# Streaming the last 96 columns of w1 beside the third block of wqkv, under a written-out order, in a transformer block with local attention and an MLP gate

## The chip, the cores and the metric

The kernel runs on one core of one Trainium2 chip. The metric is the device time of one execution in microseconds, the median over several runs. A profile of one execution comes with it: its span is the time between the first and the last thing that the profiler saw, and the time of the execution lies a little above that. The engines are TensorE (PE, with its weight loads apart as PEld), VectorE (DVE), ScalarE (ACT), GpSimd (POOL) and SyncE (SP, which here issues nearly all DMAs).

## The reference

```python
x = A_x                                   # 1 x 2048 x 512, f32
xn = layernorm(x)
qkv = (xn @ wqkv)                         # wqkv 512 x 1536; 32 heads of 16
# local attention: position s looks at s, s-2, ..., s-14 (8 offsets, dilation 2)
logits[s, w] = q[s] . k[s - 2 w] / 4      # -1e9 where s - 2 w < 0
o[s] = sum_w softmax(logits)[s, w] v[s - 2 w]
s = o @ wo                                # wo 512 x 512
y = layernorm(xn)
g = silu(gelu_tanh(y @ w1 + b1) @ w2 + b2)  # w1 512 x 1376, w2 1376 x 512
return x + s * g
```

## The kernel before, in words

**Matmuls in halves.** Each f32 factor is scaled by a power of two and split into a high and a low f16 half. A product is three f16 matmuls (high x high, low x high, high x low) summed in PSUM, over KT = 4 slices of the 512 input features: 12 matmuls for a tile of 128 tokens.

**Tokens and units.** Since the dilation is 2, even and odd positions never meet in the attention. The 2048 tokens are two parities c of 1024, each 8 tiles i of 128. The heads form NHB = 4 blocks hb of 8 heads, so wqkv falls into four blocks of 3 x 128 = 384 columns. One *unit* is a pair (c, hb): `qkv(c, hb, u)` multiplies the 8 tiles of a parity by a block of wqkv, 8 x 12 matmuls of 384 columns (L746), and ACT or DVE evicts each tile into one of two buffers U (L763, L759). SP then copies shifted rows (the halo) inside U. `attention(c, hb, u)` works on DVE with some help of POOL: multiply q with shifted k (L805), reduce (L808), softmax, multiply with shifted v (L863), sum (L858, L873, L883), scale into o (L846, L848), transposed by DMA into oT. There are eight units, four of parity 0 and four of parity 1.

**The MLP** works on four chunks ch of 512 tokens. `mlp1(ch, f)` makes 128 rows of the hidden layer for 512 tokens, f = 0 to NF - 1 = 10: 12 matmuls (L1016) with w1 as the stationary side, gelu on ACT (L1033), high half on ACT (L1036), low half on DVE (L1038). w1 has 1376 = 10 x 128 + 96 columns, so f = 10 has 96 rows (FL = 96) and goes into a tile of its own, `hlast`, whose row 97 is a constant for the bias b2. `mlp2(ch, f)` multiplies the hidden rows with w2, 4 tiles x 3 matmuls of 512 columns (L1052), summed over f in four PSUM banks z. For parity 0 the gates silu(z) go to DRAM (gd) and come back; for parity 1 they stay in U.

**The end.** wo is applied to the first three head blocks as oT comes in (L929), and for parity 1 at the end (L961). The DVE then forms gate x product (L993) and adds x (L1000, or on POOL L997), and SP writes the tile (L1002). The last tile is worked in two halves of 256 columns.

**What sets the order.** Every operation is added to a `Plan` with its engine, an estimated duration, what it reads and writes and a priority. `issue()` then picks, again and again, the operation that can start earliest, by priority among those within a small window, and emits it. The instructions of an engine, SP's DMAs among them, then run in the order in which they were emitted, each behind semaphores for what it reads. The head of the program loads x, transposed x, wqkv and the MLP weights in the order of `LOADS`; tables at the top say which engine does which cast, which tiles are transposed by DMA (`BYDMA`) or on PE (L683), and in what groups the layernorm statistics are worked (`GROUPS`).

Of the kernel before, what the change touches and what calls it, by code (L numbers as in the profile page):

```python
# [18 lines left out]
P = 128  # L19
S, D, F = 2048, 512, 1376  # L20
H, DH, W, DIL = 32, 16, 8, 2
KT = D // P
# [16 lines left out]
LAG = 2  # L39

# [4 lines left out]
BYDMA = (4, 5, 6, 7)  # L45
TRZ = (3, 3, 0, 2, 0, 1, 1, 0)
PTR = (0.5487, 0.3388, 0.0342, 0.6565, 0.7826, 0.1978, 0.0549, 0.9)
GROUPS = ((0,), (1, 2), (3, 4, 5), (6, 7))
BATCHES = ((0, 1, 2, 3, 4, 5), (6, 7))
LOADS = (('t', 6), ('q', 0), ('q', 2), ('x', 2), ('x', 0), ('q', 4), ('t', 7), ('x', 5), ('x', 1), ('x', 3), ('x', 4), ('q', 6), ('w', 0), ('w', 2), ('x', 7), ('c', 2), ('s', 1), ('c', 0), ('w', 3), ('x', 6), ('w', 1), ('c', 1), ('b', 0), ('s', 0))  # L50
HI_ENG = ('act', 'act', 'act', 'dve', 'dve', 'dve', 'dve', 'act')
XT = (0, 4, 30, 34)
Y_ENG = ('pool', 'act', 'dve', 'dve', 'act', 'pool', 'dve', 'act')

W1ENG = ('act', 'dve', 'act', 'act', 'act', 'act', 'act')
# [3 lines left out]
W2LO = ('dve', 'dve', 'dve', 'dve', 'dve', 'pool', 'dve')  # L59
EV0 = ('act', 'dve', 'dve', 'act', 'act', 'act', 'dve', 'dve')  # L60
EV1 = ('dve', 'dve', 'act', 'act', 'act', 'act', 'dve', 'act')
QLO0 = ('pool', 'dve', 'dve', 'pool')
QLO1 = ('dve', 'dve')
W1LO = ('dve', 'dve', 'pool', 'dve', 'dve', 'dve', 'dve')
WOLAG = 2
MEANBY = ('dve', 'pe', 'pool', 'pool')
W2LATE = 6

BEFORE_W1 = (0, 1, 4, 5)

# [26 lines left out]
class Plan:  # L97
# [9 lines left out]
    def add(self, eng, dur, fn, reads=(), writes=(), prio=None, table=None, nbytes=0,  # L107
            after=None, holds=(), port=False, rate=350e3, issue=0.55, tail=1.4):
# [56 lines left out]
    def start(self):  # L165
        for o in self.ops:
            o.npred, o.ready, o.succs = len(o.preds), 0.0, []
        for o in self.ops:
            for p in o.preds:
                p.succs.append(o)  # L170
        self.free = {o.eng: 0.0 for o in self.ops}
        self.portfree, self.dma, self.landed, self.table = 0.0, 0.0, [], None

    def earliest(self, o):
# [3 lines left out]
        if o.eng == "sp" and o.nbytes:  # L178
            left = FLIGHT
            for end, n in reversed(self.landed):  # L180
                left -= n
                if left < 0:
                    t = max(t, end)
                    break
        return t

    def place(self, o, t):

        if o.eng == "sp":
# [3 lines left out]
            self.dma = max(self.dma, t + o.issue + 0.3)  # L193
            self.dma += o.nbytes / (o.rate if self.dma > SLOW else 265e3)
            end = self.dma + o.tail
            self.landed.append((end, o.nbytes))
            return end
        end = t + o.dur
        if o.nbytes:
            self.free[o.eng] = end  # L200
            self.dma = max(self.dma, end + 0.3) + o.nbytes / o.rate
            return self.dma + o.tail
# [19 lines left out]
    def issue(self):  # L222
# [5 lines left out]
        order = []  # L228
        while len(order) < len(self.ops):
            best = None  # L230
            for e, cand in engs.items():
# [46 lines left out]
SLOW = 5.5  # L278

FLIGHT = 0.9e6  # L280

PW2 = 1.1284
PS2 = 0.4252
PWQ1 = 0.9
PW1 = 0.423
PB1 = 0.75
PCS = 0.6
PQ0 = 0.2677
PSQ0 = 0.1788
# [12 lines left out]
PS1 = 1.1561
# [3 lines left out]
PQLO = 0.5225  # L306

PFPLN = 0.35
PSEC = (0.6153, 0.7518, 0.1)

U1MH = 4
# [5 lines left out]
IORD0 = (6, 7, 0, 4, 1, 3, 2, 5)  # L317
IORD1 = (7, 0, 6, 3, 2, 4, 5, 1)
MLPN = (7, 7, 6, 4, 7, 7, 2, 0)
# [7 lines left out]
def tile_mixer(ctx, tc, a_x, a_xt, a_wqkv, a_wo, b_w1, b_b1, b_w2, out):  # L327
# [34 lines left out]
    ident = sb.tile([P, P], F32, name="ident")  # L362
    make_identity(nc, ident)
    fours = sb.tile([P, 2 * P], BF16, name="fours")
    nc.vector.memset(fours, 4.0)
    mean1 = sb.tile([P, P], F32, name="mean1")
# [9 lines left out]
    wq = sb.tile([P, NHB, 2, KT, 384], F16, name="wq")  # L376
    w1 = sb.tile([P, 2, KT * F], F16, name="w1")
# [6 lines left out]
    b1T = sb.tile([P, NF], F32, name="b1T")  # L384
    hlast = sb.tile([P, 2, 512], F16, name="hlast")
# [81 lines left out]
    def low_pool(n, lo, get, s, hi, **k):  # L467
# [4 lines left out]
        pool(0.45 + n * 3.9e-3, fn, **k)  # L472
# [25 lines left out]
    def k0(hb):  # L498
        return dict(rate=400e3, tail=0.6, issue=0.45) if hb == 0 else dict(tail=3.5) if hb > 1 else {}
# [9 lines left out]
    def scale_q(hb):  # L509
        col = R_s.new()  # L510
        for k in range(0, KT, 2):
            def go(k=k):
                src = stq[hb]()[:, k * 384:(k + 2) * 384]
                nc.scalar.activation(wq[:, hb, 0, k:k + 2].bitcast(BF16),
# [11 lines left out]
    def prep_q(hb):  # L526
# [3 lines left out]
        for k in range(0, KT, st):  # L530
            n = st * 384
            dst = [wq[:, hb, t, k:k + st].rearrange("p k e -> p (k e)") for t in range(2)]
            src = lambda k=k, n=n: stq[hb]()[:, k * 384:k * 384 + n]
# [17 lines left out]
    def factors(n, V, vs, mk, cdst, ckeys):  # L551
# [12 lines left out]
            rb.t[:, 0:n], p0b.t[:, 0:n], halves[:, 0:n], op=ALU.pow), [p0b], [(rb, 0)], port=False)  # L564
        with pl.fuse():
# [5 lines left out]
            cdst, a1(), halves[:, 8:8 + n], op=ALU.pow), [(A, 1)], ckeys, port=False)  # L571
# [53 lines left out]
    def ln0(g):  # L625
        q, n = cpos[g[0]], len(g)
        for i in g:
# [8 lines left out]
            rb0[:, q:q + n], pb0[:, q:q + n], halves[:, 0:n], op=ALU.pow), [("pb", g)], [("rb", g)], port=False)  # L636

    def second(g):
# [4 lines left out]
        with pl.fuse():  # L643
# [5 lines left out]
            cT[:, 0, q:q + n], x1, halves[:, 8:8 + n], op=ALU.pow), [("ab", g)], [("c", 0, i) for i in g], port=False)  # L649

    def y0(i):
# [12 lines left out]
        elif Y_ENG[i] == "pool":  # L664
            pool(1.25, lambda: nc.gpsimd.tensor_scalar(x(), x(), mv0[:, q, 0:1], rb0[:, q:q + 1], op0=ALU.subtract,
# [4 lines left out]
        if i in BYDMA:  # L670
# [6 lines left out]
                [y16, (y16, 0)] + [k for n in range(4) for k in s1k[n]], [("yh", 0, i), ("y", 0, i)], rate=140e3, issue=1.6, tail=1.2)  # L677
# [14 lines left out]
    def ln1():  # L692
# [13 lines left out]
        for i in range(NI):  # L706
# [10 lines left out]
                [y16, (y16, 0)], [("y", 1, i), ("yT", 2 + i // 4)], rate=1e6, issue=1.3)  # L717

# [646 lines left out]
```

## Time and profile before

| | before |
|---|---|
| median of 3 runs | 415.14 us (414.89 to 415.17) |
| the profiled execution | 415.18 us, span 413.4 us, mean granted clock 0.999 |
| busy: PE, DVE | 405.9 us, 379.5 us |
| busy: ACT, POOL | 222.1 us, 120.3 us |
| DMA traffic | 46.41 MB, 112 GB/s on average |
| first qkv matmul, last matmul | 15.96 us, to 409.78 us |

Busy time is the time in which an engine has an instruction under way. The chain of waits follows back from the last instruction what released it, or else the instruction ahead of it on its engine; the pieces of that chain add up to the span. In the groups, a row gives line, engine, operation, tiles and shapes, the count, then total busy time in us and mean ns, then the idle time ahead and who ended it. The table of stages gives start:end and length, the busy time of PE, PEld, DVE, ACT and POOL, the granted clock, the busy share of the DMA engines and GB/s.

### The profile page before, as it was taken

The numbers are of one execution on the slowest core, as the hardware profiler recorded it, in microseconds if no ns is written. First come the engines' busy times: TensorE is split into PE (matmuls) and PEld (weight loads), VectorE is DVE, ScalarE is ACT, GpSimd is POOL, SyncE is SP. The second block draws the span as 40 slices with busy tenths as digits, with TensorE's granted clock in tenths as the row PEclk, the third lists the DMA queues.
The fourth block names the chain that finished last, engine by engine and source line by source line (L and its number), as shares of the span: only waits on it lengthen the run. The fifth ranks groups of instructions, "written<-read, shape, count | busy, mean of one in ns | idle before, by whom it ended". The sixth has DMA issues, their size and how long they took to land.

```text
span 413.4 us, 5554 instructions
## 1 busy us (share of the span) xinstructions
PE 405.9 (98%) x2083; PEld 206.6 (50%) x2083; DVE 379.5 (92%) x379; ACT 222.1 (54%) x353; POOL 120.3 (29%) x131
## 2 busy tenths in 40 slices
PE   8799999999999999999999999999999999999996
PEld 5555544445654455445544554455455544444443
DVE  4996989998999999989998999999999998999954
ACT  4699899994549655843384252225212393263500
POOL 3834002004380425042504330434033404520021
PEclk9999999999999999999999999999999999999999
DMA  8958717030045137720172034223604244007133
GB/s 281 397 112 258 235 61 230 0 128 1 1 142 152 28 93 183 149 46 2 48 221 75 0 102 116 68 86 88 205 7 122 88 111 145 0 18 238 23 102 131
DMA packets 47211, 46.41 MB, mean 112 GB/s; under 512 B 31785, under 2 KB 32225, under 8 KB 46673
## 3 DMA queue, kind: packets, MB, share of 16 engines
q1 hardware_dynamic: 47184, 46.06, 37.6%
q8 instruction: 16, 0.26, 0.3%
q14 instruction: 11, 0.08, 0.1%
HBM read 24.06 MB, written 7.34 MB: 76 GB/s over the span
## 4 chain that ended last, share of the span: by engine, by line
PE 92%; ACT 3%; issue 1%; DVE 1%; POOL 1%; ACTq 0%
PE z L1052 28%; PE ps L1016 28%; PE ps L746 25%; PE ps L929 5%; PE ps L961 2%; PE z L961 2%; PE pl L746 1%; ACT w L421 1%; PE pl L961 1%; ACT f L673 1%; ACT yT L687 0%; ACT wq L536 0%; POOL wq L471 0%; POOL rb L635 0%; ACT prod L661 0%
## 5 line engine op out<-in xcount | busy, mean ns | idle before, releaser
L1016 PE MATMUL ps<-yT,w 128*128 128x512 f16 (+1 forms) x528 | 120.4, 379 | 0.0
L746 PE MATMUL ps<-wq,yT 128*128 128x384 f16 x708 | 117.0, 326 | 0.2 <-DVE U L759 0.2
L1052 PE MATMUL z<-w,h 128*128 128x512 f16 x480 | 110.4, 379 | 0.0
L746 PEld LDWEIGHTS <-yT 128*128 128x128 f16 x744 | 72.5, 98 | 49.2 <-issue 1.0
L1016 PEld LDWEIGHTS <-w 128*128 128x128 f16 (+1 forms) x528 | 52.8, 100 | 61.0
L805 DVE TENSOR_TENSOR prod<-U 128x2048 f32<-128x2048 f32 x32 | 73.2, 2286 | 2.2 <-POOL prod L883 0.7
L1052 PEld LDWEIGHTS <-h 128*128 128x128 f16 x480 | 46.6, 98 | 55.5 <-issue 0.3
L808 DVE TENSOR_REDUCE L<-prod 128x128 f32<-128x2048 f32 x32 | 73.0, 2281 | 0.4
L1033 ACT ACTIVATE ps<-ps,b1T,hsc 128x512 f32<-128x512 f32 (+1 forms) x44 | 32.9, 748 | 73.4 <-PE ps L1016 72.2
L863 DVE TENSOR_TENSOR prod<-pl,U 128x2048 f32<-128x2048 f32 x28 | 63.2, 2283 | 4.2 <-POOL prod L873 4.1
L763 ACT ACTIVATE U<-ps,cs 128x384 f32<-128x384 f32 x54 | 31.2, 580 | 65.2 <-PE ps L746 65.2
L873 POOL TENSOR_TENSOR prod<-prod,prod 128x2048 f32<-128x2048 f32 x7 | 31.7, 4531 | 113.8 <-DVE prod L863 99.6
L883 POOL TENSOR_TENSOR prod<-prod 128x1024 f32<-128x1024 f32 x14 | 32.9, 2349 | 0.0
L882 POOL COPY gate<-prod 1x1 f32<-1x1 f32 x21 | 5.5, 264 | 91.0 <-DVE prod L805 82.2
L1038 DVE SCALAR_TENSOR_TENSOR h<-ps,hsc,h 128x512 f16<-128x512 f32 x40 | 29.6, 741 | 1.7 <-ACT h L1036 1.4
L1036 ACT ACTIVATE h<-ps,hsc 128x512 f16<-128x512 f32 x40 | 27.3, 684 | 1.3 <-PE z L1052 0.4
L929 PE MATMUL ps<-wo,oT 128*128 128x512 f16 x96 | 21.7, 379 | 0.0
L858 DVE TENSOR_TENSOR prod<-prod,prod 128x2048 f32<-128x2048 f32 x9 | 20.5, 2282 | 0.0
L1033 ACT ACT_TABLE_LOAD x10 | 12.8, 1283 | 8.6 <-PE ps L1016 8.5
L883 POOL TENSOR_TENSOR prod<-prod,prod 128x1024 f32<-128x1024 f32 x7 | 16.4, 2347 | 0.0
L961 PEld LDWEIGHTS <-oT 128*128 128x128 f16 x108 | 10.6, 98 | 10.4
L929 PEld LDWEIGHTS <-oT 128*128 128x128 f16 x96 | 9.4, 98 | 11.2
(179 smaller groups left out, 377.8 us busy)
## 6 DMA issues: line engine op xcount, KB each, us to landing
f<-in_A_x_dram SPq DMA_DIRECT2D x31, 256.0 KB, 3.5
U<-U SPq DMA_DIRECT2D x16, 392.0 KB, 4.0
gd<-f SPq DMA_DIRECT2D x12, 256.0 KB, 3.4
prod<-in_A_x_dram SPq DMA_DIRECT2D x8, 256.0 KB, 6.9
oT<-in_B_w_dram SPq DMA_DIRECT2D x2, 1024.0 KB
yT<-in_B_w_dram SPq DMA_DIRECT2D x2, 1024.0 KB, 7.9
f<-gd SPq DMA_DIRECT2D x8, 256.0 KB, 2.7
out_dram<-f SPq DMA_DIRECT2D x8, 256.0 KB, 2.8
```

Source lines behind the costliest of these rows:

```text
L746: nc.tensor.matmul(b.t[:, 0:384], y[:, s, k, o:o + P], wq[:, hb, t, k], start=(n == 0), stop=(n == 11))
L763: act(384, lambda i=i, b=b: nc.scalar.activation(U3[:, i:i + 31:15, :], b.t[:, 0:384].rearrange("p (t e) -> p t e", t=3), AF.Identity, sca ...
L805: dve(2048, lambda p2=p2, g=g: nc.vector.tensor_tensor(p2(), q, slots(Ut, KH, 2 * g), op=ALU.mult), qk + [("kh", ub, 0), ("kh", ub, 1), (" ...
L808: dve(2048, lambda pr=pr, g=g: nc.vector.tensor_reduce(L3()[:, 2 * g:2 * g + 2], pr.t.rearrange("p (r f d) -> p r f d", r=2, d=DH), AX.X, ...
L863: dve(2048, lambda: nc.vector.tensor_tensor(pr.t.rearrange("p (r f d) -> p r f d", r=2, d=DH), A3()[:, 2 * g:2 * g + 2].rearrange("p r (f ...
L873: pool(4.75, lambda: nc.gpsimd.tensor_tensor(acc.t, acc.t, p1.t, op=ALU.add), [acc, p1], [acc])
L883: nc.gpsimd.tensor_tensor(x.t[:, 0:1024], x.t[:, 0:1024], y(), op=ALU.add)
L929: nc.tensor.matmul(b.t, oT[:, hb, i // 4, s, i % 4], wo[:, t, hb], start=(hb == 0 and n == 0), stop=(hb == last and n == 2))
L961: nc.tensor.matmul(b.t[:, cols], oT[:, hb, i // 4, s, i % 4], wo[:, t, hb, cols], start=(start and hb == 0 and n == 0), stop=(stop and hb ...
L1016: nc.tensor.matmul(b.t[0:M], w1[:, s, f * 512 + k * M:f * 512 + (k + 1) * M], yT[ch][:, t, k], start=(n == 0), stop=(n == 11))
L1033: act(512, lambda: nc.scalar.activation(b.t[0:M], b.t[0:M], AF.Gelu_apprx_tanh, bias=b1T[0:M, f:f + 1], scale=hsc[0:M, 1:2]), [b, ("b1T",) ...
L1052: nc.tensor.matmul(z.t, hl[s][0:K, t * P:(t + 1) * P], w2[0:K, w, f], start=(f == 0 and n == 0), stop=(f == NF - 1 and n == 2))
```

## The change

The hidden rows of f = 10 are no longer made by `mlp1`. The last 96 columns of w1 lie beside block hb = 2 of wqkv (`HLAST = 2`), and where `qkv` works on that block, its matmuls stream 480 columns instead of 384. The 96 extra columns come out with tokens on partitions. ACT evicts them separately, `last_block` adds the bias (a row broadcast over partitions, for which b1T has 96 more columns), does gelu and the two halves, and a transposing DMA brings them into the form that `mlp2` reads:

```diff
-    wq = sb.tile([P, NHB, 2, KT, 384], F16, name="wq")
-    w1 = sb.tile([P, 2, KT * F], F16, name="w1")
+    wq = [sb.tile([P, 2, KT, 384 + FL * (hb == HLAST)], F16, name=f"wq{hb}") for hb in range(NHB)]
+    w1 = sb.tile([P, 2, W1C[3]], F16, name="w1")
+    wl = wq[HLAST][:, :, :, 384:384 + FL]
...
+    def last_block(ch):
+        n = 4 * FL
...
+        x = hpt[j][:, 0:n]
...
+            pool(0.9, pads, [("hsc2",), ("hp", j, 0), ("hp", j, 1)], [(h16, 2)], port=False)
+            pool(1.0, lambda: nc.gpsimd.tensor_tensor(x3(), x3(), row, op=ALU.add), xk + [("b1T",)], xk)
+            act(n, lambda: nc.scalar.activation(x, x, AF.Gelu_apprx_tanh), xk, xk,
+                aps=1, table="gelu")
+            act(n, lambda: nc.scalar.activation(v()[:, 0, :, 0:FL], x3(), AF.Identity, scale=hsc[:, 2:3]),
+                xk + [("hsc2",)], [(h16, 0)])
+            dve(n, lambda: nc.vector.scalar_tensor_tensor(v()[:, 1, :, 0:FL], x3(), hsc[:, 2:3], v()[:, 0, :, 0:FL],
+                                                          op0=ALU.mult, op1=ALU.subtract),
...
+            dma(P * 2048, lambda: nc.sync.dma_start_transpose(dst, h16.t.bitcast(F16)), [(h16, k) for k in range(3)],
...
     def qkv(c, hb, u):
...
+        wide = 384 + FL * (hb == HLAST)
...
-                    nc.tensor.matmul(b.t[:, 0:384], y[:, s, k, o:o + P], wq[:, hb, t, k],
+                    nc.tensor.matmul(b.t[:, 0:wide], y[:, s, k, o:o + P], wq[hb][:, t, k],
...
+            if hb == HLAST:
+                act(FL, lambda i=i, b=b: nc.scalar.activation(
+                    hpt[i // 4][:, (i % 4) * FL:(i % 4 + 1) * FL], b.t[:, 384:384 + FL], AF.Identity, scale=hsc[:, 1:2]),
...
+        for j in range(2 if hb == HLAST else 0):
+            last_block(2 * c + j)
...
-            if p < len(steps):
+            if p < len(steps) and steps[p][1] < NF - 1:
```

Units run in the order parity 0, hb = 0 to 3, then parity 1, so the wide units are the third and the seventh. `hlast` and the POOL operations for its last row go.

The second part is the order. `issue()` takes the operations from a table `ORDER` of 1260 operation numbers, and its own choice is made only when the table is used up:

```diff
+ORDER = (
+    2, 1, 4, 0, 116, 127, 131, 126, 128, 112, 111, 132, 115, 121, 120, 25, 110, 118, 125, 123, 129, 26, 27, 122,
...
-        order = []
+        order, fixed = [], [self.ops[n] for n in reversed(ORDER)]
...
+            if fixed:
+                o = fixed.pop()
...
-LOADS = (('t', 6), ('q', 0), ('q', 2), ('x', 2), ('x', 0), ('q', 4), ('t', 7), ('x', 5), ('x', 1), ('x', 3), ('x', 4), ('q', 6), ('w', 0), ('w', 2), ('x', 7), ('c', 2), ('s', 1), ('c', 0), ('w', 3), ('x', 6), ('w', 1), 
+LOADS = (('t', 6), ('q', 0), ('t', 7), ('q', 2), ('x', 0), ('x', 5), ('x', 2), ('q', 4), ('x', 1), ('q', 6), ('x', 4), ('x', 3), ('x', 6), ('w', 0), ('w', 2), ('x', 7), ('c', 2), ('w', 1), ('c', 1), ('w', 3), ('b', 0), 
-BYDMA = (4, 5, 6, 7)
+BYDMA = (2, 5, 6, 7)
-GROUPS = ((0,), (1, 2), (3, 4, 5), (6, 7))
+GROUPS = ((0,), (1,), (2, 3, 4), (5,), (6, 7))
-Y_ENG = ('pool', 'act', 'dve', 'dve', 'act', 'pool', 'dve', 'act')
+Y_ENG = ('act', 'dve', 'act', 'dve', 'act', 'act', 'dve', 'act')
-MEANBY = ('dve', 'pe', 'pool', 'pool')
+MEANBY = ('pe', 'pe', 'pe', 'dve')
```

Other tables of engines and priorities change in the same manner. The engines' counts: PE loses 48 matmuls, DVE gains 2 rows, ACT 15, POOL 14, SP 4 (the transposes).

**SP at the head of the program**, where U and prod hold transposed x, x and the blocks of wqkv as they arrive. Before:

```order
L1124 DMA U_87<-in_A_xt_dram 128x512
L505 DMA prod_93<-in_A_wqkv_dram 128x768 x2
L1099 DMA prod_94<-in_A_x_dram 128x512 x2
L505 DMA U_87<-in_A_wqkv_dram 128x768
L1124 DMA U_87<-in_A_xt_dram 128x512
L1099 DMA prod_95<-in_A_x_dram 128x512
L1099 DMA prod_94<-in_A_x_dram 128x512 x2
L1099 DMA prod_95<-in_A_x_dram 128x512
```

After:

```order
L1231 DMA U_89<-in_A_xt_dram 128x512
L577 DMA prod_95<-in_A_wqkv_dram 128x768
L1206 DMA prod_96<-in_A_x_dram 128x512
L1231 DMA U_89<-in_A_xt_dram 128x512
L1206 DMA prod_96<-in_A_x_dram 128x512
L1206 DMA prod_97<-in_A_x_dram 128x512
L577 DMA prod_95<-in_A_wqkv_dram 128x768
L1206 DMA prod_97<-in_A_x_dram 128x512
```

The second piece of wqkv moves from the third transfer to the seventh.

**DVE where the attention of the first unit begins** (L805 and L912 are the same multiply, L808 and L915 the same reduction, L1038 and L1141 the low half of a hidden block h). Before:

```order
L805 TENSOR_TENSOR prod_94<-U_86 128x2048
L759 TENSOR_SCALAR U_87<-ps_141,cs_114 128x3x128
L808 TENSOR_REDUCE L_103<-prod_94 128x2x64
L805 TENSOR_TENSOR prod_93<-U_86 128x2048
L1038 SCALAR_TENSOR_TENSOR h_107<-ps_139,hsc,h_107 128x512
L1038 SCALAR_TENSOR_TENSOR h_108<-ps_140,hsc,h_108 128x512
L808 TENSOR_REDUCE L_103<-prod_93 128x2x64
L1038 SCALAR_TENSOR_TENSOR h_106<-ps_141,hsc,h_106 128x512
```

After:

```order
L912 TENSOR_TENSOR prod_95<-U_88 128x2048
L915 TENSOR_REDUCE L_105<-prod_95 128x2x64
L912 TENSOR_TENSOR prod_96<-U_88 128x2048
L912 TENSOR_TENSOR prod_97<-U_88 128x2048
L1141 SCALAR_TENSOR_TENSOR h_109<-ps_143,hsc,h_109 128x512
L511 TENSOR_REDUCE s_125<-z_145 128x1
L513 TENSOR_SCALAR s_125<-s_125 128x1
L520 TENSOR_SCALAR s_126<-s_125 128x1
L526 TENSOR_SCALAR zsc<-s_126 128x1
L531 TENSOR_SCALAR zsc<-s_126 128x1
L1141 SCALAR_TENSOR_TENSOR h_110<-ps_141,hsc,h_110 128x512
```

The first hidden block stands behind two multiplies and one reduction before, with its second neighbour right behind it, and behind three multiplies and a reduction after, with the second block behind five short operations for the scale of w2 (L511 to L531).

**SP at the end** (L983 and L1090 load x, L851 and L958 transpose o into oT, L972 and L1079 bring gates back, L1002 and L1109 write tiles of parity 1, L1030 one of parity 0). Before:

```order
L983 DMA U_86<-in_A_x_dram 128x512 [waits DMAHW3_49]
L851 DMA_TRANSPOSE oT<-o_105 128x8x128 [waits DMAHW4_49,DVE_49]
L851 DMA_TRANSPOSE oT<-o_105 128x8x128 [waits DMAHW5_49,DVE_49,PE_49]
L1002 DMA out_dram<-U_86 128x512 [waits DMAHW6_49,Pool_49]
L1002 DMA out_dram<-U_86 128x512 [waits DMAHW7_49,Pool_49]
L1002 DMA out_dram<-U_86 128x512 [waits DMAHW0_49,DVE_49]
L1002 DMA out_dram<-U_86 128x512 [waits DMAHW1_49,DVE_49]
L1002 DMA out_dram<-U_86 128x512 [waits DMAHW2_49,Pool_49]
L1002 DMA out_dram<-U_86 128x512 [waits DMAHW3_49,DVE_49]
L1002 DMA out_dram<-U_86 128x512 [waits DMAHW4_49,DVE_49]
L1002 DMA out_dram<-U_86 128x256 [waits DMAHW5_49,DVE_49]
L1002 DMA out_dram<-U_86 128x256 [waits DMAHW6_49,DVE_49]
```

After:

```order
L958 DMA_TRANSPOSE oT<-o_107 128x8x128 [waits DMAHW7_49,DVE_49,PE_49]
L1090 DMA f_99<-in_A_x_dram 128x512 [waits DVE_49]
L1109 DMA out_dram<-U_88 128x256 [waits DMAHW1_49,DVE_49,Activation_49]
L1109 DMA out_dram<-U_88 128x512 [waits DMAHW2_49]
L1109 DMA out_dram<-U_88 128x512 [waits DMAHW3_49]
L1109 DMA out_dram<-U_88 128x512 [waits DMAHW4_49]
L1030 DMA out_dram<-f_104 128x512 [waits DMAHW5_49]
L1109 DMA out_dram<-U_88 128x512 [waits DMAHW6_49,Pool_49]
L1109 DMA out_dram<-U_88 128x512 [waits DMAHW7_49]
L1109 DMA out_dram<-U_88 128x512 [waits DMAHW0_49]
L1109 DMA out_dram<-U_88 128x512 [waits DMAHW1_49,Pool_49]
L1109 DMA out_dram<-U_88 128x256 [waits DMAHW2_49,DVE_49]
```

The half tiles (128x256) are the two halves of the last tile: the first of them, which waits for DVE and ACT, stood next to last and now stands ahead of all other outputs; DVE's add for it is the row before the last on that engine, behind the evict of the last matmuls.

More of the change, by code (lines that the diff above doesn't have):

```diff
@@ L178, in earliest @@
         if o.eng == "sp" and o.nbytes:
[L179 to L184, printed above, removed]
+            if len(self.landed) >= FLIGHT:
+                t = max(t, self.landed[-FLIGHT])
         return t
```

206 lines of the change are left out of this document (113 added, 93 removed), and 60 rows, old and new, of the table ORDER.

## The prediction

> **What bounds the kernel now.** I read the page first, then the chain of waits, then who waits for whom, then the stages, and last the end of the timeline. The first lines of the page, and its summary of the chain:
>
> ```profile
> span 413.4 us, 5554 instructions
> PE 405.9 (98%) x2083; PEld 206.6 (50%) x2083; DVE 379.5 (92%) x379; ACT 222.1 (54%) x353; POOL 120.3 (29%) x131
> PE 92%; ACT 3%; issue 1%; DVE 1%; POOL 1%; ACTq 0%
> ```
>
> TensorE is the bound. A busy share alone would not show it, since matmuls are pipelined and DVE is at 92% too; the chain does: 92% of the span hangs on PE. Pieces of the chain, in order of time (start, length, what):
>
> ```profile
> 46.38 10.36 PE ps L1016 x48
> ...
> 101.60 15.60 PE ps L746 x96
> ...
> 399.37 9.08 PE z L961 x48
> ```
>
> 48 matmuls of 512 columns take 10.36 us, 215.9 ns each; 96 of 384 columns take 15.60 us, 162.5 ns each. What PE waits for over the whole span:
>
> ```profile
> PE z L683 <- POOL prod L665: 1.6, 1, 1.6
> PE z L1169 <- DVE fours L365: 1.2, 1, 1.2
> PE z L683 <- DVE prod L668: 0.4, 1, 0.4
> PE ps L746 <- DVE U L759: 0.2, 1, 0.2
> ```
>
> All of it lies in the head. From the stages (start:end, length, then busy time of each engine):
>
> ```profile
> 52.00:95.00 43.00, 43.00 (x207) 19.80 (x206) 41.72 (x50) 39.24 (x73) 4.25 (x9) 1.00 0.30 100
> 95.00:336.00 241.00, 240.96 (x1260) 123.71 (x1259) 231.57 (x183) 115.05 (x169) 78.45 (x80) 1.00 0.33 89
> ```
>
> PE is full in both, at granted clock 1.00, but DVE has only 1.28 us left of 43, and 9.4 of 241. So PE work taken away is time gained up to the point at which PE runs into DVE. The end, from the timeline:
>
> ```profile
> 406.10 5.01 SPq L1002 DMA_DIRECT2D out_dram<-U  x4
> 408.29 1.47 PE L961 MATMUL ps<-wo,oT 128*128 128x256 f16 x12
> 409.80 0.48 DVE L993 SCALAR_TENSOR_TENSOR U<-ps,osc,U 128x256 f32<-128x256 f32 x1 [0.29 <-PE ps L961]
> 410.32 0.42 DVE L1000 TENSOR_TENSOR U<-U 128x256 f32<-128x256 f32 x1
> 399.60 11.50 SPq L1002 DMA_DIRECT2D out_dram<-U  x9
> ```
>
> PE ends at 408.29 + 1.47 = 409.76, two DVE operations follow to 410.74, the last output is issued up to 399.60 + 11.50 = 411.10, and the span ends at 413.4: 3.6 us after the last matmul. The nine outputs of the second parity are spread over 11.5 us, each behind its own add, so only the last of them counts.
>
> The profiled execution took 415.18 us for a span of 413.4, 1.78 outside; the median of the runs is 415.14, so I add 1.78 to a span. About 0.2% (0.8 us) is what a measurement of this kernel can tell from no change.
>
> **The change part by part.** *Matmuls.* The block f = 10 of the first MLP product is removed; its rows, and those of the qkv product that become wider:
>
> ```profile
> L1016 PE MATMUL ps<-yT,w 128*96 128x512 f16 x48 | 11.0, 379 | 0.0
> L746 PE MATMUL ps<-wq,yT 128*128 128x384 f16 x708 | 117.0, 326 | 0.2 <-DVE U L759 0.2
> ```
>
> Gone: 48 x 215.9 ns = 10.36 us. Added: two units of 8 tiles x 12 matmuls = 192, 384 to 480 columns. No 480-wide matmul is in the trace; the two pitches above give (215.9 - 162.5)/128 = 0.417 ns a column, so 192 x 96 x 0.417 ns = 7.69 us. The dear end is the price of a full 512 columns, 192 x 53.4 ns = 10.25. A cheap end lies little under 7.69: two widths fix the slope, and a curve that bent would have to bend between them; I allow 7.5. I take 7.7, on the line between the neighbours: **-2.7 us**, ends -2.9 and -0.1.
>
> *The head.* The order replaces the way into the first product:
>
> ```profile
> 6.84 0.84 ACT L514 ACTIVATE wq<-prod 128x768 bf16<-128x768 f32 x1 [1.41 <-DMA prod<-in_A_wqkv_dram]
> 8.92 2.13 ACT L536 ACTIVATE wq<-prod,qsc 128x384 f16<-128x384 f32 x4 [1.15 <-DVE qsc L459]
> 15.96 0.81 PE L746 MATMUL ps<-wq,yT 128*128 128x384 f16 x4
> 17.84 1.85 PE L683 MATMUL z<-ident,prod 128*128 128x128 f32 x12 [0.40 <-DVE prod L668]
> 8.00:20.00 12.00, 9.75 (x54) 6.15 (x55) 11.35 (x39) 7.49 (x15) 8.16 (x9) 1.00 1.04 410
> ```
>
> In before the second half of the first weight block is the third transfer and is squared at 6.84; its scale lets ACT start at 8.92. After, it is the seventh: four tiles of 262 KB more ahead of it, at 410 GB/s 2.6 us later, so the scale comes near 11.5. Following the new order with the durations of these rows, the first qkv matmul starts at 16.6 instead of 15.96. But by then 12 of the 16 transposes on PE are done (before: 4), so 8 x 1.85/12 = 1.2 us less PE work lies behind it, and the two normalizations on POOL, of which one held PE 1.6 us, are on ACT and DVE. The means made on PE instead of DVE, the other tiles that are transposed by DMA and the new groups of statistics act in this stretch alone and are in the 16.6. The PE work from the first qkv matmul to the last matmul, all by the pitches above, is 392.4 us in before and, by 392.4 - 2.7 - 1.2 and 0.2 for small sums that move, 388.7 after. Before: 15.96 + 392.4 + 1.4 of waits = 409.76, as measured. After: 16.6 + 388.7 = 405.3 plus waits g. The 16.6 is an estimate and may be 1 off either way.
>
> *Waits g.* Before had 1.4. On equal work the new order is 17.4 - 15.6 = 1.8 us sooner on PE after the head (15.96 + 1.4 against 16.6 - 1.2 + 0.2). It takes that into the 52 to 95 stage where DVE has 1.28 us to spare, and each gelu block passes through DVE:
>
> ```profile
> L1038 DVE SCALAR_TENSOR_TENSOR h<-ps,hsc,h 128x512 f16<-128x512 f32 x40 | 29.6, 741 | 1.7 <-ACT h L1036 1.4
> L863 DVE TENSOR_TENSOR prod<-pl,U 128x2048 f32<-128x2048 f32 x28 | 63.2, 2283 | 4.2 <-POOL prod L873 4.1
> ```
>
> A block behind one attention multiply waits 2.28 us. So I expect what the head gains to be given back there. A second place is the last unit's qkv, now interleaved with MLP blocks and done only near 337, about when DVE wants it. I take g = 2.0, ends 0 (nothing waits) and 4.5 (two blocks, each behind one such multiply).
>
> *The last block's small operations* are hidden. For four chunks:
>
> ```profile
> L763 ACT ACTIVATE U<-ps,cs 128x384 f32<-128x384 f32 x54 | 31.2, 580 | 65.2 <-PE ps L746 65.2
> L1036 ACT ACTIVATE hlast<-ps,hsc 96x512 f16<-96x512 f32 x4 | 2.7, 680 | 0.1
> L1038 DVE SCALAR_TENSOR_TENSOR hlast<-ps,hsc,hlast 96x512 f16<-96x512 f32 x4 | 3.0, 744 | 1.9 <-ACT hlast L1036 1.9
> L471 POOL TENSOR_TENSOR wq<-prod,wq 128x384 f16<-128x384 f32 x2 | 1.9, 928 | 0.2
> ```
>
> 16 more ACT evictions of 96 columns (at most 0.58 us each, the 384-column price: 9.3 us) and 8 ACT operations of 384 for 8 of 512; ACT is at 115 of 241 us in that stage. On DVE four operations of 384 columns replace four of 512, a gain under 0.6. POOL gets four adds of about 0.93 and four pads; it is at 78 of 241. Four transposes join SP. With that cover gone, the block would stand between the qkv unit and one chunk's last product: an add, two ACT operations, one on DVE and a transpose, near 6 us once. It isn't gone: the chunk's product is placed tens of microseconds later.
>
> *The tail* decides. In the new order of SP, the output of the last tile's first half stands **ahead of nine others**: seven second-parity tiles, a first-parity tile and the second half. SP takes its instructions in order (so does every engine here), and that first one waits for the DVE add which itself stands behind the evict of the very last matmul. So all ten, 8 x 262 KB + 2 x 131 KB = 2.36 MB, leave only then. Prices:
>
> ```profile
> 372.19 3.70 SPq L983 DMA_DIRECT2D f<-in_A_x_dram  x7
> out_dram<-U SPq DMA_DIRECT2D x7, 256.0 KB, 2.0
> out_dram<-U SPq DMA_DIRECT2D x2, 128.0 KB, 1.7
> ```
>
> Start: last matmul + 0.04 + 0.48 (evict) + 0.42 (add) + 0.06 = T_P + 1.0. Seven issues back to back took 3.70 us, 0.53 each, so the tenth starts 9 x 0.53 = 4.8 us later. From its issue to the span's end there were 411.10 - 0.33 = 410.77 to 413.4, 2.6 us. By issue alone: T_P + 8.4 (7.7 if an issue took the 0.45 of a lone one). By data: 256 KB lands in 2.0 and 128 KB in 1.7, so some 1.4 us is fixed; 2.36 MB at the 410 GB/s seen above is 5.8 us; with 0.9 from the last landing to the end that is T_P + 9.1. I take T_P + 8.7, ends 7.7 and 9.8 (350 GB/s): **+5.1 us** against 3.6.
>
> On the drain the Trainium skill speaks in "DMA: Bandwidth & Descriptors", section "Bandwidth": transfers between HBM and SBUF are held at about 358 GB/s for a core. The 410 GB/s row disagrees for loads; no row shows a run of writes of this length. By the page the drain would be 6.6 us and the sum 0.8 longer.
>
> The page's section "Anatomy of one DMA" gives a fixed 2.0 us a transfer, most of it the receipt of the write, heaviest into HBM. The rows here show 1.7 us in all for 128 KB into HBM, so I keep 1.4; by the page the tail would be 0.6 longer.
>
> **Sum.** T_P = 405.3 + 2.0 = 407.3 (before 409.76). Span 407.3 + 8.7 = 416.0, execution 417.8; with g at before's 1.4 it is 417.2. I forecast **417.5 us**, +2.4.
>
> **Rivals.**
> *A, the forecast:* PE gains 2 to 4 us, the outputs held back lose 4 to 6. 415.9 to 419.
>
> *B, faster:* the held outputs cost next to nothing, because the queue in front of the chip accepts them early and only the last piece counts. Then 407.3 + 3.6 + 1.78 = 412.7. For it: outputs so far land 2 us after issue however many there are. Against it: in before no output was issued ahead of its own wait, and 2.36 MB need 5.8 us at any rate seen. It decides once the tail is under 7.2 us at g = 0 (405.3 + 7.2 + 1.78 = 414.3).
>
> *C, about even:* g near 0 and the tail at its lower end: 405.3 + 7.7 + 1.78 = 414.8.
>
> *D, PE runs into DVE:* the interleaved qkv tiles and MLP blocks make PE wait in many places, g = 4.5 or more, beside the tail: 405.3 + 4.5 + 8.7 + 1.78 = 420.3.
>
> *E, the change doesn't save on PE:* a 480-wide matmul costs what a 512-wide one does; 2.6 more, 420.1.
>
> **How the numbers follow.** A 0.57, B 0.12, C 0.11, D 0.15, E 0.05. Faster by more than 0.2% is B, 0.12; within it C, 0.11; slower A, D and E, 0.77. The range takes C's low end less the 1 us of the head, 413.8, and D with a tail of 9.8, 421.3; what is left out is most of B and what g could be beyond that.
>
> **What would show it.** Right: in the new profile the last PE matmul near 407; on SP one unbroken row of ten output issues, starting a microsecond after it; nothing on the output queue in the ten microseconds before; the 480-wide pieces at about 202.6 ns each; first qkv matmul near 16.6; PE waits of a few tenths each on DVE between 50 and 100 us. Wrong: outputs issued before the last matmul; a span that ends under 6 us after it; PE pieces at 216 ns for 480 columns; or long PE waits past 100 us.

## The result, and the profile after

The kernel became slower by more than forecast: 429.97 us (428.74 to 430.77, four runs) against 415.01 (414.81 to 415.17), a ratio of 1.0358 with a 95% interval of 1.0331 to 1.0386. The forecast was 417.5, range 413.8 to 421.3. The profiled execution of the changed kernel took 429.54 us for a span of 427.8. The first lines of its page, and the summary of its chain of waits:

```profile
span 427.8 us, 5487 instructions
PE 405.5 (95%) x2041; PEld 201.3 (47%) x2041; DVE 390.3 (91%) x381; ACT 220.7 (52%) x368; POOL 136.5 (32%) x145
PE 51%; DVE 29%; issue 8%; DMA 5%; ACT 2%; SPq 2%; POOL 1%; DVEq 0%; ACTq 0%; POOLq 0%
```

Before, 92% of the chain hung on PE and 1% on DVE; now 51% and 29%. DVE's busy time rose from 379.5 to 390.3 us for two more rows. Two pieces of the chain, the first qkv matmul and a run of 480-column matmuls:

```profile
16.86 0.76 PE ps L846 x4
272.34 12.15 PE ps L846 x60
```

12.15 us for 60 is 202.5 ns each. What PE waits for from then on (engine, what it makes, on whom; total, times, longest), 10.3 us in all, where before had 0.6:

```profile
PE ps L846 <- DVE h L1141: 2.7, 3, 1.8
PE z L1159 <- DVE h L1141: 2.2, 1, 2.2
PE ps L1123 <- DVE f L1050: 2.2, 2, 1.4
PE z L507 <- ACT w L493: 1.4, 1, 1.4
PE ps L1123 <- DVE h L1141: 0.8, 2, 0.5
PE ps L1123 <- ACT U L864: 0.4, 1, 0.4
PE ps L846 <- DVE f L1050: 0.4, 1, 0.4
PE ps L846 <- DVE ssq L513: 0.2, 1, 0.2
```

The prediction's own sign of being wrong, long PE waits past 100 us, is in this list: 2.2 us between 140 and 145, 1.8 between 190 and 195, and 2.6 in three pieces between 310 and 325.

The stages (start:end, length, busy PE, PEld, DVE, ACT, POOL, clock, DMA share, GB/s):

```profile
52.00:95.00 43.00, 40.57 (x191) 18.11 (x190) 40.42 (x44) 31.22 (x52) 14.78 (x13) 1.00 0.21 63
95.00:240.00 145.00, 140.03 (x712) 69.11 (x710) 139.62 (x113) 86.91 (x152) 51.87 (x49) 1.00 0.40 97
240.00:336.00 96.00, 93.45 (x467) 45.50 (x466) 93.02 (x67) 30.53 (x50) 35.39 (x40) 1.00 0.36 88
```

PE was full in all of them before; now it has gaps in each, at the same granted clock of 1.00. The end, from the timeline (start, length, what), and what SP waited for ahead of its first row there:

```profile
416.48 1.47 PE L1068 MATMUL ps<-wo,oT 128*128 128x256 f16 x12
418.40 0.75 DVE L1107 TENSOR_TENSOR U<-U 128x256 f32<-128x256 f32 x2
418.88 1.80 SPq L1109 DMA_DIRECT2D out_dram<-U  x4
420.72 0.46 SPq L1030 DMA_DIRECT2D out_dram<-f  x1
421.27 3.26 SPq L1109 DMA_DIRECT2D out_dram<-U  x5
```

```profile
SPq L1109 <- DVE U L1107: 10.0, 1, 10.0
```

The ten outputs leave in one row from 418.88, as the order said. In two stretches behind that the busy share of the DMA engines and the GB/s (the last two columns) are those of a full queue:

```profile
420.00:422.00 2.00, 0.00 (x0) 0.00 (x0) 0.00 (x0) 0.00 (x0) 0.00 (x0) 1.00 0.99 363
422.00:424.00 2.00, 0.00 (x0) 0.00 (x0) 0.00 (x0) 0.00 (x0) 0.00 (x0) 0.80 1.03 383
```

In the prediction's own sum the 14.4 us of span are: the first qkv matmul 0.9 later (16.86 for 15.96), PE work 3.7 less, waits g of 12.4 instead of 1.4, and a tail of 9.8 instead of 3.6 (427.8 - 417.96). The last matmul ends at 417.96, and 417.96 - 16.86 - 388.7 is the 12.4. The 1.4 of before is such a difference too; its list names 0.6. After, the list names 10.3; for the rest PE is recorded as busy, 390.8 us from the first qkv matmul to the last matmul where 388.7 was worked out, and what lengthened it is not shown.

Where DVE's 10.8 us come from, the groups show (count, total busy us, mean ns, idle ahead). After:

```profile
L912 DVE TENSOR_TENSOR prod<-U 128x2048 f32<-128x2048 f32 x32 | 77.9, 2438 | 1.7 <-DMA U<-U 0.7
L785 DVE TENSOR_TENSOR f<-f,f 128x512 f16<-128x512 f32 x8 | 13.5, 1683 | 0.4 <-ACT f L784 0.4
L980 POOL TENSOR_TENSOR prod<-prod,prod 128x2048 f32<-128x2048 f32 x7 | 37.5, 5354 | 70.2 <-DVE prod L970 70.2
```

Before, the two DVE operations, the subtraction that makes parity 1's low half (now L785) and the q times k multiply (now L912):

```profile
L713 DVE TENSOR_TENSOR f<-f,f 128x512 f16<-128x512 f32 x8 | 6.5, 810 | 0.0
L805 DVE TENSOR_TENSOR prod<-U 128x2048 f32<-128x2048 f32 x32 | 73.2, 2286 | 2.2 <-POOL prod L883 0.7 <-DMA U<-U 0.3
```

The same counts and shapes take 7.0 and 4.7 us longer; all other DVE rows together are 0.9 us shorter. A mean that rises on unchanged work says that single instructions were held. The timeline of DVE and POOL at two such places:

```profile
133.91 2.28 DVE L912 TENSOR_TENSOR prod<-U 128x2048 f32<-128x2048 f32 x1
134.07 6.49 POOL L980 TENSOR_TENSOR prod<-prod,prod 128x2048 f32<-128x2048 f32 x1 [8.14 <-DVE prod L970]
136.58 4.53 DVE L785 TENSOR_TENSOR f<-f,f 128x512 f16<-128x512 f32 x1 [0.39 <-ACT f L784]
...
304.25 4.51 POOL L980 TENSOR_TENSOR prod<-prod,prod 128x2048 f32<-128x2048 f32 x1 [3.38 <-DVE prod L970]
304.75 6.16 DVE L912 TENSOR_TENSOR prod<-U 128x2048 f32<-128x2048 f32 x1
```

At 304.25 POOL's long addition is under way alone, 4.51 us, and the DVE multiply that starts behind it ends 2.15 us (its own 2.28) after POOL's end. At 134.07 it is POOL that starts second, beside a multiply, and takes 6.49; the next subtraction is then held in its turn, 4.53 us instead of about 0.7. Each such lock-out costs DVE 3.8 to 3.9 us, and there are three (133 to 141, 181, 305). A fourth, shorter one stands at 73 us, beside a POOL operation on 512 elements a partition:

```profile
72.57 1.65 POOL L543 TENSOR_TENSOR w<-f,w 128x512 f16<-128x512 f32 x1
73.12 3.25 DVE L912 TENSOR_TENSOR prod<-U 128x2048 f32<-128x2048 f32 x1
```

The multiply takes 1.0 us more than its 2.28 there. No experiment takes this one away.

The Trainium skill has this rule in "SBUF — State Buffer", section "Who interferes with whom": a DVE operation with two inputs in SBUF and a GpSimd instruction that reads SBUF exclude each other for a whole instruction, and whichever came first finishes. The rows above agree: 4.53 and 6.16 us for DVE behind POOL, 6.49 for POOL behind DVE.

### The profile page after: what moved, and what is told of

It reads as the page before. It is cut to its first block, busy times and chain, and to the rows that moved or that the text cites. A ratio compares the mean times of both kernels' runs of the same rounds, so it can differ in the third digit from the quotient of the medians.

```text
span 427.8 us, 5487 instructions
## 1 busy us (share of the span) xinstructions
PE 405.5 (95%) x2041; PEld 201.3 (47%) x2041; DVE 390.3 (91%) x381; ACT 220.7 (52%) x368; POOL 136.5 (32%) x145
## 4 chain that ended last, share of the span: by engine, by line
PE 51%; DVE 29%; issue 8%; DMA 5%; ACT 2%; SPq 2%; POOL 1%; DVEq 0%; ACTq 0%; POOLq 0%
PE ps L846 19%; PE z L1159 12%; PE ps L1123 11%; DVE prod L970 7%; DVE prod L912 6%; DVE L L915 5%; PE ps L1036 3%; DVE h L1141 3%; DMA yT<-in_B_w_dram 2%; PE ps L1068 2%; PE z L1068 2%; DVE prod L965 2%; DMA prod<-in_A_wqkv_dram 1%; DMA prod<-in_A_x_dram 1%; DVE w L558 1%
## 5 line engine op out<-in xcount | busy, mean ns | idle before, releaser
L846 PE MATMUL ps<-wq,yT 128*128 128x384 f16 (+1 forms) x720 | 130.3, 337 | 3.3 <-DVE h L1141 2.7
L1159 PE MATMUL z<-w,h 128*128 128x512 f16 x480 | 112.8, 379 | 2.2 <-DVE h L1141 2.2
L1123 PE MATMUL ps<-yT,w 128*128 128x512 f16 x480 | 109.9, 379 | 3.4 <-DVE f L1050 2.2
L912 DVE TENSOR_TENSOR prod<-U 128x2048 f32<-128x2048 f32 x32 | 77.9, 2438 | 1.7 <-DMA U<-U 0.7
L1123 PEld LDWEIGHTS <-w 128*128 128x128 f16 x480 | 46.8, 98 | 61.5 <-issue 6.4
L915 DVE TENSOR_REDUCE L<-prod 128x128 f32<-128x2048 f32 x32 | 72.9, 2283 | 0.6
L980 POOL TENSOR_TENSOR prod<-prod,prod 128x2048 f32<-128x2048 f32 x7 | 37.5, 5354 | 70.2 <-DVE prod L970 70.2
L1136 ACT ACTIVATE ps<-ps,b1T,hsc 128x512 f32<-128x512 f32 x40 | 29.6, 747 | 36.7 <-PE ps L1123 36.6
L1141 DVE SCALAR_TENSOR_TENSOR h<-ps,hsc,h 128x512 f16<-128x512 f32 x40 | 29.4, 742 | 4.5 <-ACT h L1139 4.5
L953 ACT ACTIVATE o<-prod,osc 128x1024 f16<-128x1024 f32 (+1 forms) x9 | 9.5, 1053 | 19.5 <-DVE prod L965 11.9
L1068 PEld LDWEIGHTS <-oT 128*128 128x128 f16 x108 | 10.6, 98 | 10.4
```

The costliest lines, as they stand in the source:

```text
L846: nc.tensor.matmul(b.t[:, 0:wide], y[:, s, k, o:o + P], wq[hb][:, t, k], start=(n == 0), stop=(n == 11))
L912: dve(2048, lambda p2=p2, g=g: nc.vector.tensor_tensor(p2(), q, slots(Ut, KH, 2 * g), op=ALU.mult), qk + [("kh", ub, 0), ("kh", ub, 1), (" ...
L915: dve(2048, lambda pr=pr, g=g: nc.vector.tensor_reduce(L3()[:, 2 * g:2 * g + 2], pr.t.rearrange("p (r f d) -> p r f d", r=2, d=DH), AX.X, ...
L980: pool(4.75, lambda: nc.gpsimd.tensor_tensor(acc.t, acc.t, p1.t, op=ALU.add), [acc, p1], [acc])
L1123: nc.tensor.matmul(b.t[0:M], w1[:, s, f * 512 + k * M:f * 512 + (k + 1) * M], yT[ch][:, t, k], start=(n == 0), stop=(n == 11))
L1136: act(512, lambda: nc.scalar.activation(b.t[0:M], b.t[0:M], AF.Gelu_apprx_tanh, bias=b1T[0:M, f:f + 1], scale=hsc[0:M, 1:2]), [b, ("b1T",) ...
```

## The experiments

My theory after the comparison had two parts that should add up: the outputs held behind the last tile (about 6 us), and DVE locked out by POOL's long addition (most of g). The rivals were that PE would only find the next wait when either went, and that the new layout itself, not the order, is what costs.

**The outputs, undone.** Each of the ten outputs is put right behind its own add in the table:

```diff
+MOVED = ((1225, 1224), (1235, 1216), (1245, 1244), (880, 1216), (1220, 1219), (1230, 1229),
+         (1250, 1249), (1240, 1239), (1255, 1254), (1259, 1258))
+for _out, _add in MOVED:
+    ORDER.remove(_out)
+    ORDER.insert(ORDER.index(_add) + 1, _out)
```

> The changed kernel with one thing moved: each of the ten last outputs is issued right behind the add that makes its tile, instead of behind the add of the last tile's first half; engines, matmuls and the rest of the table stay. Theory A (the tail is an own term, paid in full): the distance from the last matmul to the end of the span falls from 9.8 us to that of the kernel before, 3.6 us, the last matmul stays near 418; time 430.0 - 6.2 = 423.8, range 422.5 to 425. Rival B (the outputs are limited by something else at the end, such as the adds on DVE and POOL behind PE): gain under 2 us, 428 or more.

Measured: 424.04 us (423.85 to 425.71), ratio to before 1.0221 [1.0197, 1.0245], 5.9 less than the changed kernel. The SP row at the end:

```profile
409.15 10.36 SPq L1116 DMA_DIRECT2D out_dram<-U  x9
```

Nine outputs are spread over 10.4 us again. The last matmul ends at 417.78, as with the table untouched, and the span of 422.1 is 4.3 beyond it, where 3.6 was expected.

**The outputs alone, put into before.** Eight of before's nine last outputs are issued behind the ninth:

```diff
+        held = (1232, 1197, 1202, 1207, 1212, 1217, 1222, 1227)
+        order = ([x for x in order if x[1].n not in held] +
+                 [x for n in held for x in order if x[1].n == n])
```

> The kernel before with one thing moved: eight of its nine last outputs are issued behind the very last one, so all nine (2.1 MB) leave after the last add. Theory A (an own term of the tail: issues 0.45 to 0.53 us apart, or 2.1 MB at 410 GB/s): the last matmul stays at 409.8, the end comes 4 to 5 us later, 419 to 420. Rival B (outputs drain behind other work or faster than seen): under 2 us more, 415 to 417.

Measured: 420.21 us (419.87 to 420.32), ratio 1.0117 [1.0099, 1.0135], 5.3 more than before. Its end on SP, and the drain:

```profile
410.49 4.76 SPq L1005 DMA_DIRECT2D out_dram<-U  x9
...
412.00:414.00 2.00, 0.00 (x0) 0.00 (x0) 0.00 (x0) 0.00 (x0) 0.00 (x0) 0.68 0.98 360
414.00:416.00 2.00, 0.00 (x0) 0.00 (x0) 0.00 (x0) 0.00 (x0) 0.00 (x0) 0.50 1.02 379
```

So the row of outputs costs 5 to 6 us in either kernel, and nothing else of the change is needed for it.

**Two of the three lock-outs.** POOL first reads one element of what the DVE operation makes, so that the long addition can't begin before it has ended. The kernel has the same kind of copy ahead of its shorter additions; the long one had none. HOLD names by their numbers in the table the addition and the DVE operation that it is held behind:

```diff
+HOLD = {469: 343, 947: 1065}
...
+            if o.n in HOLD:
+                self.hold(self.ops[HOLD[o.n]].bufs[-1].t)
             o.fn()
...
+    pl.hold = lambda x: nc.gpsimd.tensor_copy(gate, x[0:1, 256:257])
```

> The changed kernel with two tiny reads more on POOL: ahead of the long add of the second unit, POOL reads one element of what DVE's low half of the parity-1 layernorm tile writes (the operation that took 4.53 instead of 0.69 us), and ahead of that of the sixth unit one element of what DVE's multiply writes (6.16 instead of 2.28). So POOL starts its add only behind them, as the planner had assumed. Theory A (POOL's add, when it starts first, locks DVE's two-operand operations out, and TensorE pays for it later): both DVE operations fall to 0.7 and 2.3 us, 7.7 us of DVE time, and the last matmul comes 4 to 7 us sooner; time 423 to 426. Rival B (DVE would have waited there for something else anyway, or TensorE is held by other things): DVE operations shorter, time within 1.5 us of 430. Rival C (the lock has nothing to do with who starts first): the two operations stay long.

Measured: 423.67 us (422.4 to 424.28), ratio 1.0199 [1.0176, 1.0222], 6.3 less than the changed kernel. The timeline at the first place:

```profile
135.94 0.69 DVE L789 TENSOR_TENSOR f<-f,f 128x512 f16<-128x512 f32 x1 [0.39 <-ACT f L788]
136.69 0.18 POOL L900 COPY gate<-f 1x1 f32<-1x1 f32 x1 [11.41 <-DVE f L789]
136.83 4.52 POOL L985 TENSOR_TENSOR prod<-prod,prod 128x2048 f32<-128x2048 f32 x1
137.21 2.28 DVE L920 TENSOR_REDUCE L<-prod 128x128 f32<-128x2048 f32 x1
139.52 4.49 DVE L975 TENSOR_TENSOR prod<-pl,U 128x2048 f32<-128x2048 f32 x2
```

The subtraction takes 0.69 us again, for a copy of 0.18 on an engine with room. The addition now lies beside a reduction and two multiplies with one operand in PSUM (pl), and those keep their 2.28 and 2.24 us each: only DVE operations with two SBUF operands were held. At the second place the multiply takes 2.28 us again. In PE's list the 2.2 us on h, and the 2.2 and 0.4 on f, are gone, and the last matmul ends at 411.76, 6.2 sooner.

**Both together.**

> Both edits at once: the ten last outputs right behind their adds, and POOL's two long adds held behind the DVE operations that they had locked out. Theory A (two separate terms, one at the end and one in the middle): the gains of 5.9 and 6.3 us add up, 430.0 - 12.2 = 417.8, range 416.8 to 418.8. Rival B (they overlap, since the outputs drain while TensorE would wait): 420 or more.

Measured: 417.69 us (416.54 to 417.84), ratio 1.0064 [1.0047, 1.0081]. 5.9 and 6.3 add up to 12.2; together they gave 12.3. So the two terms add up, and 2.6 us over before were left.

**The layout without the table.** ORDER is empty, so that the program's own planner orders the changed layout:

> The changed kernel's layout, load order, engines and priorities, without the table: every operation is placed by the planner's own choice, which keeps DVE's and POOL's two-operand work apart by its estimates and issues outputs when they are ready. Theory A (the table is what costs: outputs 6.2, lock-outs and late inputs about 10): 412 to 419. Rival B (the wide third block with its extra evictions, bias adds and transposes is what costs): 425 or more, with the 2.7 us fewer matmuls eaten up.

Measured: 419.41 us (418.85 to 419.81), ratio 1.01 [1.0082, 1.0118]; 10.6 less than with the table, 4.5 more than before, and just above theory A's range. The two DVE groups that had grown are nearly back here: the multiply has a mean of 2295 ns (2438 with the table), the subtraction one of 928 (1683). PE has one wait that the table avoids, 1.5 us for the last block's transpose; the rest of the 4.5 us is not taken apart.

**The layout with before's constants** as well as no table:

> The wide third block alone: the changed layout with the engines, loads and priorities of the kernel before, and no table, so the planner places everything as it did before. Theory A (the layout saves 2.7 us of matmuls, and its small operations hide): 411 to 414, faster than before. Rival B (the last block's chain of POOL, ACT, DVE and a transpose, and a chunk that can't end before the third unit, hold TensorE): 416 or more.

Measured: 431.18 us (428.19 to 432.0), ratio 1.0374 [1.0337, 1.0412]. This told nothing on the layout: before's constants place the head badly for it (the first attention multiply starts at 55.3 us, 43.4 with the table), and one wait of 5.7 us stands alone there.

**The w2 loads.** The first hidden block of the changed kernel, from the timelines of SP, ACT and DVE:

```profile
41.74 0.57 SPq L1237 DMA_DIRECT2D yT<-in_B_w_dram  x1
...
51.99 1.91 ACT L493 ACTIVATE w<-yT 128x2048 bf16<-128x2048 f32 x1 [1.52 <-DMA yT<-in_B_w_dram]
53.89 0.67 ACT L1139 ACTIVATE h<-ps,hsc 128x512 f16<-128x512 f32 x1
...
54.60 0.75 DVE L1141 SCALAR_TENSOR_TENSOR h<-ps,hsc,h 128x512 f16<-128x512 f32 x1 [2.17 <-ACT h L1139]
```

The second 1 MB piece of w2 is issued at 41.74. ACT stands 1.52 us for it, squares it for 1.91, and only then makes the half that DVE wants. The edit, on top of both, puts the two pieces earlier in SP's row:

```diff
+         (107, 98), (105, 163))
```

> The same with both edits, and the two 1 MB loads of w2 earlier on SP: the first right behind the last transpose of the first layernorm (about 33.5 us instead of 40.4), the second ahead of the small copy that it followed. Theory A (ACT stood idle 3.4 us for these loads with the first hidden blocks queued behind it, and TensorE waited 2.6 us for that between 49 and 56 us): the loads land some 5 us sooner, these waits go, time 2 to 3 us below that of the two edits alone, 414.8 to 416. Rival B (the wait comes back as the halo copies or DVE's first multiply become late, or DVE is the bound there anyway): within 1 us of the two edits alone.

Measured: 416.16 us (415.52 to 416.84), ratio 1.0023 [1.0013, 1.0032]. They are issued at 32.60 and 39.70, and 1.5 us go, less than expected.

**Is DVE's place or DVE's load what is left?** Some operations that stood ahead of blocks h on DVE are moved behind them, on top of the last kernel:

```diff
+         (382, 479), (733, 732), (734, 733), (615, 734), (1254, 1253))
```

> The kernel with the outputs at their adds, the two held adds of POOL and the earlier w2 loads, and three small moves more: on DVE the low half of the first hidden block goes ahead of the third multiply of the first unit (TensorE waited 1.28 us for it at 53 us) and that of a later hidden block goes ahead of a multiply and a subtraction (1.68 us at 190), and at the end the add of the last tile's first half goes ahead of the evict of its second half (0.4 us). Theory A (each hidden block behind a multiply costs TensorE what it waits there, and nothing takes it up later): 416.2 - 1.3 - 1.7 - 0.3 = 412.9, range 412.4 to 414.5, faster than the kernel before (415.1). Rival B (the evict and the multiply that stand behind them now become late, and TensorE waits there instead): 415 or more.

Measured: 416.54 us (415.83 to 416.97), ratio 1.0039 [1.0025, 1.0053]: no gain. Two waits of 1.3 and 1.7 us went, and four of 0.4 to 1.2 came in other places. To see the load, the first reduction of units 1 and 2 is cut to 2 of its 16 products:

```diff
+                (pr.t[:, 0:256] if lean else pr.t).rearrange("p (r f d) -> p r f d", r=2, d=2 if lean else DH),
```

> The kernel with the outputs at their adds, the two held adds of POOL and the earlier w2 loads (416.2 us), with less work on DVE: the first reduction of the first unit and of the second unit sums 2 of 16 products instead of all 16, so its output differs there; everything else, the order too, is the same. It takes about 1.9 us off DVE near 46 us and again near 100 us. Theory A (between 50 and 232 us DVE is the bound, and the 4.4 us that TensorE still waits there are DVE's lateness): waits of 1.3, 0.3, 0.7 and 1.7 us go or shrink, time 412 to 414.5. Rival B (TensorE waits for the place of single operations in the order, not for DVE's load, as the move of three of them might still allow): under 1 us less, 415.2 or more.

Measured: 413.02 us (412.73 to 414.0), ratio 0.9962 [0.9949, 0.9974], 3.1 less. Two reductions of 0.42 us stand for two of 2.28, 3.7 us of DVE taken away:

```profile
L929 DVE TENSOR_REDUCE L<-prod 128x128 f32<-128x256 f32 x2 | 0.8, 416 | 0.0
```

After 30 us PE's list has one row left, where the kernel without the cut has 4.4 us in all:

```profile
PE ps L858 <- DVE h L1156: 1.9, 2, 1.7
```

The waits ahead of 100 us are gone; 1.7 at 190 and 0.3 at 227 stay. So what the cut acted on lies ahead of 100 us, and the two later waits have another cause. The lock-out at 176 us (below) is still in this kernel.

The same edit on before:

> The kernel before with the same two reductions shortened. There TensorE waits for nothing after 31 us, so by theory A DVE's time is not on the path: within 0.6 us of the kernel before, 414.5 to 415.7. If DVE bound that kernel as well, it would be 2 to 4 us faster.

Measured: 415.19 us (414.89 to 416.18), ratio 1.0008 [0.9999, 1.0017]. Nothing. So DVE's time in that stretch is worth about 0.8 us for each us in the changed kernel with these edits, and nothing in before: the bound has moved there.

**The third lock-out.** I had left one in place at 176 us. In the kernel with the earlier w2 loads:

```profile
176.03 4.50 POOL L993 TENSOR_TENSOR prod<-prod,prod 128x2048 f32<-128x2048 f32 x1 [12.87 <-DVE prod L983]
176.46 4.62 DVE L797 TENSOR_TENSOR f<-f,f 128x512 f16<-128x512 f32 x1
```

```diff
-HOLD = {469: 343, 947: 1065}
+HOLD = {469: 343, 613: 368, 947: 1065}
```

> The kernel with the outputs at their adds, two held adds of POOL and the earlier w2 loads (416.2 us), and a third add of POOL held in the same way: that of the third unit, which began 0.4 us ahead of a DVE subtraction of the layernorm of parity 1 (4.62 instead of 0.69 us, at 176 us). Theory A (DVE is the bound up to 232 us): 3.9 us off DVE take the TensorE waits behind it (1.7 at 190, 0.3 at 227) away, 416.2 - 2.0 = 414.2, range 413.2 to 414.8, below the kernel before. Rival B (the waits at 190 come from the place of the hidden block's operation alone): within 0.7 us of 416.2.

Measured: 414.41 us (413.56 to 415.15, twelve runs), ratio 0.9987 [0.9975, 0.9999]: 1.8 less. It is 0.5 under before, which is inside the 0.2% that the prediction took as even. The same subtraction, and the stage:

```profile
176.70 0.68 DVE L797 TENSOR_TENSOR f<-f,f 128x512 f16<-128x512 f32 x1
...
95.00:240.00 145.00, 144.85 (x745) 72.65 (x745) 137.43 (x115) 87.25 (x152) 53.71 (x61) 1.00 0.39 93
```

PE is full again: the waits at 190 and 227 are gone, and what it still waits after 30 us, 2.4 in all, lies ahead of 96 us.

**The last, with two of the moves that had gained nothing:**

```diff
+         (382, 479), (1254, 1253))
```

> The same with the low half of the first hidden block ahead of the first unit's third multiply, and the last tile's first add ahead of its second evict. With DVE's load as the bound up to 100 us, the first move takes 1.3 us at 53 us away and gives most of it back in the next blocks, as it did before: 0 to 1 us; the second gains 0.3 at the end. Expected 413.2, range 412.4 to 414.3. Rival: no gain or a loss from the first move, 414.2 or more.

Measured: 414.42 us (413.9 to 416.69), ratio 0.9989 [0.9976, 1.0002]. No further gain.

## Why the prediction was right or wrong

**Right: what bounds before, the matmuls, the head.** 202.5 ns for 480 columns, forecast 202.6; rival E is out. The first qkv matmul came at 16.86 where 16.6 was worked out; over the kernels with the table, which share the rows up to there, it lies between 15.7 and 16.9, inside the 1 us allowed; that the one run came within 0.3 us is partly luck. With the three lock-outs and the wait for w2 taken away and 2.4 us of waits left, the last matmul ends at 407.97 (before 409.78), and PE is busy 389.3 us from the first qkv matmul on, forecast 388.7: the gain of the layout on PE is there.

**Right in mechanism, at the end of its range: the tail.** 8.7 was forecast, between a sum by issue (8.4) and one by data (9.1), ends 7.7 and 9.8; it measured 9.8, and undoing it was worth 5.9. The mis-sized piece is the drain: I took 410 GB/s from a stretch of loads, and the writes went at 363 to 383, by which the sum by data is 9.5 to 9.8. The upper end was added up wrong: with 350 GB/s that sum gives 10.0. The Trainium skill's 358 GB/s ("DMA: Bandwidth & Descriptors", section "Bandwidth"), which I set aside, was the nearer. The 2.0 us a transfer that the prediction quotes from the section "Anatomy of one DMA" are given there for DMAs that GpSimd issues, and SyncE issues these; the forecast did not use them. Rival B, by which early issues are accepted ahead of the wait, is out: SP stood 10.0 us behind one add.

**Right: the last block's small operations are hidden.** No wait of PE on them stands in the list with the table; one of 1.5 us does without it.

**Wrong: the waits g, 2.0 forecast, ends 0 and 4.5, 12.4 measured.** The step that failed is "two blocks, each behind one such multiply" as the upper end. It took DVE's durations from the groups of before as fixed and asked only in which order they stand. The runs put three things in its place, 8.1 and 1.5 us of time and 2.4 us of waits, together 12.0 for the 12.4:

- POOL's long addition and DVE's two-operand operations exclude each other. Taking the three lock-outs away was worth 6.3 and 1.8, 8.1 us together; with them gone DVE's busy time is 379.0 us instead of 390.3. The prediction had an answer for POOL's busy time (78 of 241 us) and none for when it is busy. The hint was in before's own groups: L713 has a mean of 810 ns because one of its eight took 1.52 us at 140.32, beside a POOL addition that ran from 136.74 to 141.29, where the median is 0.68: one lock-out in small.
- The w2 pieces come late in SP's row, ACT stands for them, and DVE behind ACT: 1.5 us. I had followed SP's queue at the head and the tail, and not between.
- DVE is then late up to 96 us with 2.4 us of waits. This is the part that I had forecast as "given back there", at about its size. The short lock-out is still in that stretch (with all three others gone it holds a subtraction of 0.68 us for 1.55 near 71 us) and may be part of it; no run tells.

Rival D named the right direction, PE running into DVE, at 420.3 and a chance of 0.15. It had g = 4.5, from the order alone.

Why the table brings POOL and DVE together is not shown by a run; that it does is, since without it the two groups have nearly the means of before. What the runs also show is that an order fixes the row on each engine and not the time between two engines. The kernel with only the outputs moved has the changed kernel's rows up to its tail, and yet near 71 us it held a subtraction (1.63 us instead of 0.68) where the changed kernel held the multiply behind it. The long addition starts as soon as its operands are there, and a copy of 0.18 us that makes it wait is enough.

From 429.97: the outputs and two lock-outs to 417.69, the w2 loads to 416.16, the third lock-out to 414.41. That is 0.5 below before's 414.89 in the same runs, with an interval that ends just under 1, and within the 0.2% taken as even. So nearly all of the 15 us lay in the order of the table and in when POOL starts, and the layout, with its new tables of loads and engines, is worth no more than about half a microsecond as yet. Its last matmul comes 1.8 us sooner than in before, but the tail behind it is 4.3 us instead of 3.6. What stays open is whether the 2.4 us ahead of 96 us can go: moving operations about did not do it, and taking DVE work away did.

## What to carry to other kernels

In this kernel a fixed order per engine did not settle which instructions of two engines lay beside each other: where two engines can exclude each other, compare the mean of each group with that of the kernel before, look at the timeline where it rose, and hold the long instruction back with a tiny one that reads what should come first. A spare of a few per cent on DVE was no cover here once PE had less to do; whether that is so can be tried by cutting a little of the second engine's work in both kernels and seeing which of them answers. In the row of a DMA queue, look for the issue whose wait ends last and count what stands behind it.

## What the runs showed of the hardware that I had not expected

- A DVE operation on 512 elements a partition, 0.69 us alone, took 4.53 and 4.62 beside a POOL addition of 2048; a reduction, and a multiply with an operand in PSUM, kept their time beside the same addition.
- It goes both ways: the addition took 4.5 us when it came first and 6.49 when a DVE multiply of 2.28 was under way.
- Writes of 256 KB back to back left at 360 to 383 GB/s with the DMA engines full, below the 410 of the loads at the start.
